# Forty scatters of a routed feed-forward layer, each to a view of its own

## The chip, the cores and the metric

The kernel runs on one core of a Trainium2 chip. The metric is the time of one execution on the device, in microseconds (us). Three runs of the kernel before took 685.83, 689.69 and 692.70 us; the median is 689.69 us. One further execution was profiled and took 693.05 us, of which the profile shows a span of 691.3 us.

The engines are PE (TensorE, matmul), ACT (ScalarE), DVE (VectorE), POOL (GpSimd) and SP (SyncE). POOL also issues every transfer whose addresses come from a table of indices, and one instruction after the other in the order in which the program has them.

## The reference

Attention comes first, for 8 batches of 8 heads, with 512 local queries (a band of 32 keys to either side and the 32 global keys) and 32 global queries. Its output is a matrix x of 4608 rows and 512 columns. Then each row goes to one of 8 experts:

```python
logits = x @ w_gate
# (row, expert) pairs in falling order of their logit: a row goes to the first
# expert that still has room; each expert takes cap = 4608 // 8 = 576 rows
for e in range(E):
    mask = assigned == e
    h = np.maximum(x[mask] @ w1[e], 0.0)     # 512 -> 1024
    out[mask] = h @ w2[e]                    # 1024 -> 512
```

Each row of `out` belongs to one expert, so the rows that two experts write are never the same, nor those of two tiles of one expert.

## The kernel before, in words

The first part, up to about 200 us, is attention; x goes to a buffer `xd` in DRAM. Then the rows of the first expert are chosen, and from about 238 us on the experts follow one after another. The experts are called phases 0 to 7 here, in the order in which they are worked on.

A phase has an H part and a Y part on PE. The H part (`ffn`, line 1127) multiplies the expert's 576 rows by W1: 16 pieces of 12 matmuls, each operand split in a high and a low half. ACT takes the relu (1129, 1131) and DVE the low half of it (`hl`, issued by line 1134 and recorded at 552). The Y part multiplies by W2: a tile of 32 rows (`rest_out`, 1094) and four tiles of 128 rows (`rows_out`, 1086). In phase 7 the small tile comes last, in the other phases first.

Each of the five tiles of a phase ends in `out_tile` (1069): ACT copies the sum to a buffer `y` (1074), and a scatter from POOL (`scatter`, 973 to 976) writes its rows to `out`, by a column of the table `idx`. So there are 8 x 5 = 40 scatters. The tiles of 128 rows are called s0 to s3 in this text. The 32-row tile is written as 128 pieces of 128 columns to `out4`, which is `out` seen as four times as many rows, a quarter as long.

POOL's other transfers in this part are gathers, all at line 918: the 576 rows of the next phase (`xg`, five of them), and its weights (`w1r` and `w2r`, two of 1 MB each). For each phase they stand in POOL's order so: five `xg`, two `w2r`, s0 to s3, two `w1r` for the phase after. At the turn from phase 5 to phase 6 it is different: s0, s1, the two `w1r` of phase 7, s2, s3, and then the five `xg` of phase 7.

The order on each engine is fixed when the program is built. The kernel counts a reckoned clock (`V.now`) along with PE's work, and a list `todo` holds jobs that are put into the program at the first step where that clock is late enough:

```python
def put():
    scatter(ph, t, y)
    wrote[0] = pool_op(1040, sizes[t] * 2048) + LAND
at("out", V.now + 900, put, lambda: V.now >= wrote[0])
```

So a scatter gets a place behind the point where the one before it is reckoned to have landed. Nothing of this runs on the chip. What runs there are waits on semaphores, which the program's dependency tracker adds: a scatter waits for the ACT copy of its own `y`, and, since all 40 write to one tensor with rows known only at run time, for the landing of a scatter before it.

Transfers issued by POOL count on eight semaphores in turn, DMASW0 to DMASW7. A transfer also waits until the last one on its own semaphore, eight transfers earlier, has landed, unless a wait before it already covers that.

Of the kernel before, what the change touches and what calls it, by code (L numbers as in the profile page):

```python
# [7 lines left out]

F32 = mybir.dt.float32
F32R = mybir.dt.float32r  # L10
# [11 lines left out]
E = 8  # L22
# [23 lines left out]
@with_exitstack  # L46
def block(ctx, tc, A, out, nbatch=B, dump=None):
    nc = tc.nc
    ctx.enter_context(tc.manual_schedule())
    consts = ctx.enter_context(tc.tile_pool(name="consts", bufs=1))  # L50
    dram = ctx.enter_context(tc.tile_pool(name="dram", bufs=1, space=DRAM))
    xd = dram.tile([N, DM], F32, name="xd")

    ident = consts.tile([128, 128], F32, name="ident")
    L = consts.tile([128, 34, E], F32, name="L")
    if dump is not None:
        nc.vector.memset(L, 0.0)
    rt = Routing(tc, A, consts, L, ident) if out is not None else None
    if rt:
        rt.begin(ctx)  # L60
    attention(tc, A, consts, xd, ident, L, nbatch, rt)
    if dump is not None:
        nc.sync.dma_start(dump["L"], L.rearrange("p a b -> p (a b)"))
        nc.sync.dma_start(dump["x"][:nbatch * S], xd[:nbatch * S])
    if out is not None:
        rt.begin_ps(ctx)
        experts(tc, A, xd, ident, rt, out)
# [830 lines left out]
def experts(ctx, tc, A, xd, ident, rt, out):  # L898
    nc = tc.nc
# [10 lines left out]
    hh = wp.tile([128, 8, CAP], F32R, name="hh")  # L910
    hl = wp.tile([128, 8, CAP], F32R, name="hl")
    h32 = wp.tile([128, 8, 32], F32, name="h32")
    out4 = out.rearrange("n (c d) -> (n c) d", c=4)
    sizes = [128, 128, 128, 128, 32]
    HF = CAP // 2

# [55 lines left out]

    def scatter(ph, t, y):
        k = t + (t == 4)
        nc.gpsimd.indirect_dma_start(out=out4 if t == 4 else out, out_offset=bass.IndirectOffsetOnAxis(  # L975
            ap=rt.idx[ph][:, k:k + 1], axis=0), in_=y, in_offset=None)

    V = rt.V
# [90 lines left out]
    def out_tile(ph, t, p):  # L1069
        while len([x for x in todo if x[0] == "out"]) > 3:  # L1070
            force("out", 1)
        w = 128 if t == 4 else DM
        y = st.tile([128, w], F32, name=f"y{w}", bufs=4 if w == DM else 2)
        nc.scalar.activation(y, p[:, :w], AF.Copy)  # L1074
# [5 lines that stand above are left out]
# [217 lines left out]
```

## Time and profile before

| | |
|---|---|
| median of 3 runs | 689.69 us (685.83 to 692.70) |
| profiled execution, own time | 693.05 us |
| its span | 691.3 us |
| PE busy | 644.5 us (93%) |
| DVE busy | 460.0 us (67%) |
| ACT busy | 307.4 us (44%) |
| POOL busy | 247.7 us (36%) |
| the 40 scatters, on POOL | 41.4 us, with 183.3 us of idle time ahead of them |

A chain of waits is followed back from the last instruction, and it gives PE 89% of the span. The idle time ahead of the scatters is POOL's own, and says nothing yet about PE. A wait for several semaphores is put down to the engine that came last by the profile, which is not always the one that was waited for: whoever reads a scatter's wait has to look at when its own `y` was ready.

### The profile page before, as it was taken

Reading aid. Unit: us, or ns where it says so; the run is one execution under the profiler, and the core shown is the slowest. Engines: PE = TensorE matmul, PEld = TensorE weight load, DVE = VectorE, ACT = ScalarE, POOL = GpSimd, SP = SyncE. Lnnn points to the kernel's source line nnn. Section 1 sums busy time; section 2 is a strip of 40 time slices with the busy share of each in tenths; the row PEclk is TensorE's granted clock in tenths of the full one; section 3 lists DMA queues with packets and bytes.
Section 4 is the critical chain, followed back from the end, with each engine's and each line's share of the span. In section 5 each row is a group of like instructions: output and inputs, shape, how many; then the busy total and the mean of one; then the engine's idle time right before and its main releaser. Section 6 shows DMA issues by size and latency. Waiting matters only on the chain.

```text
span 691.3 us, 24695 instructions
## 1 busy us (share of the span) xinstructions
PE 644.5 (93%) x10358; PEld 539.5 (78%) x10358; DVE 460.0 (67%) x1765; ACT 307.4 (44%) x828; POOL 247.7 (36%) x313
## 2 busy tenths in 40 slices
PE   7898999999973799999999999999999999999996
PEld 6576777776762698779879879878978978988985
DVE  4688888788776699778758758767767772640410
ACT  5777867876720252443433324334333342542410
POOL 4687767786500311511421331141151133412011
PEclk9999999999985799999999999999999999999999
DMA  8677778876210531713240450361343146431001
GB/s 252 192 241 221 228 227 249 256 212 185 90 68 2 186 124 42 287 47 109 84 168 18 153 190 33 126 197 53 122 125 129 45 142 214 163 127 49 14 15 51
DMA packets 41119, 93.91 MB, mean 136 GB/s; under 512 B 5424, under 2 KB 28208, under 8 KB 36912
## 3 DMA queue, kind: packets, MB, share of 16 engines
q0 software_dynamic: 10240, 51.39, 21.5%
q1 hardware_dynamic: 30768, 40.95, 19.5%
q8 instruction: 81, 1.33, 0.8%
q14 instruction: 30, 0.25, 0.1%
HBM read 74.49 MB, written 17.83 MB: 134 GB/s over the span
## 4 chain that ended last, share of the span: by engine, by line
PE 89%; DVE 4%; issue 3%; DMA 2%; ACT 1%; SPq 0%; POOL 0%; POOLq 0%; ACTq 0%
PE H L1127 28%; PE Y L1086 27%; PE T L90 11%; PE S L90 7%; PE O L90 7%; PE R L630 4%; PE H L965 2%; PE Y L1094 2%; DMA qk<-in_qk_dram 1%; DVE r_pm L552 1%; DMA mask<-in_mask_dram 1%; DMA xg<-xd,idx 0%; DVE r_G L552 0%; DVE r_ce L552 0%; DMA out_dram<-y,idx 0%
## 5 line engine op out<-in xcount | busy, mean ns | idle before, releaser
L1127 PE MATMUL H<-xh,w1h 128*128 128x272 f32 (+2 forms) x512 | 151.1, 295 | 2.4 <-ACT xh L970 2.0
L1127 PE MATMUL H<-xh,w1l 128*128 128x272 f32 (+2 forms) x512 | 150.4, 294 | 0.0
L1127 PE MATMUL H<-xl,w1h 128*128 128x272 f32 (+2 forms) x512 | 149.7, 292 | 0.1
L975 POOL DMA_INDIRECT out_dram<-y,idx x40 | 41.4, 1036 | 183.3 <-ACT y L1074 102.8
L1086 PE MATMUL Y<-w2l,hh 128*128 128x512 f32 x256 | 103.3, 403 | 0.8 <-issue 0.8
L1129 ACT ACTIVATE hh<-H 128x272 fp32r<-128x272 f32 (+2 forms) x128 | 50.8, 398 | 119.7 <-PE H L1127 117.0
L1086 PE MATMUL Y<-w2h,hh 128*128 128x512 f32 x256 | 104.0, 406 | 0.0
L1086 PE MATMUL Y<-w2h,hl 128*128 128x512 f32 x256 | 103.4, 404 | 0.0
L1127 PEld LDWEIGHTS H<-xh,w1h 128*128 128x128 f32 x512 | 97.0, 189 | 3.9 <-ACT xh L970 2.1
L1127 PEld LDWEIGHTS H<-xl,w1h 128*128 128x128 f32 x512 | 97.0, 189 | 1.0 <-DVE xl L552 0.4
L1127 PEld LDWEIGHTS H<-xh,w1l 128*128 128x128 f32 x512 | 97.0, 189 | 0.4
L126 POOL COPY vw<-vw 32x650 f32<-32x650 f32 x96 | 69.4, 723 | 51.6 <-DMA vw<-in_vw_dram 36.1
L180 ACT ACTIVATE p<-p,nm 128x128 f32<-128x128 f32 x256 | 78.0, 397 | 8.1 <-DVE nm L175 8.1
L1074 ACT ACTIVATE y<-Y 128x512 f32<-128x512 f32 (+1 forms) x40 | 21.3, 534 | 123.7 <-PE Y L1086 80.3
L552 DVE SCALAR_TENSOR_TENSOR hl<-H,hh 128x272 fp32r<-128x272 f32 (+2 forms) x128 | 55.1, 434 | 30.3 <-ACT h L1131 18.5
L175 DVE CUSTOM_DVE_ANT_0 p<-S,mask 128x128 f32<-128x128 f32 x256 | 56.5, 286 | 23.3 <-PE S L90 21.8
L90 PE MATMUL S<-qk 64*32 64x128 f32 (+2 forms) x2240 | 52.6, 293 | 9.5 <-issue 5.1
L552 DVE TENSOR_TENSOR w2l<-w2r,w2h 128x512 fp32r<-128x512 f32 x64 | 42.8, 682 | 25.3 <-ACT w2h L931 25.3
L918 POOL DMA_INDIRECT xg<-xd,idx x40 | 43.3, 1082 | 38.1 <-DVE idx L552 23.8
L1086 PEld LDWEIGHTS Y<-w2h,hh 128*128 128x128 f32 x256 | 48.2, 188 | 10.4 <-issue 1.4
L1086 PEld LDWEIGHTS Y<-w2h,hl 128*128 128x128 f32 x256 | 48.2, 188 | 9.8 <-issue 0.5
L1086 PEld LDWEIGHTS Y<-w2l,hh 128*128 128x128 f32 x256 | 48.2, 188 | 9.5 <-issue 0.4
(179 smaller groups left out, 1116.9 us busy)
## 6 DMA issues: line engine op xcount, KB each, us to landing
qk<-in_qk_dram SPq DMA_DIRECT2D x64, 204.0 KB, 2.9
vw<-in_vw_dram SPq DMA_DIRECT2D x64, 162.5 KB, 3.4
xd<-xs SPq DMA_DIRECT2D x28, 256.0 KB, 3.5
qk<-in_qk_dram SPq DMA_DIRECT2D x32, 200.0 KB, 3.0
xd<-xs SPq DMA_DIRECT2D x1, 1024.0 KB
xg<-xd,idx POOLq DMA_INDIRECT x40
out_dram<-y,idx POOLq DMA_INDIRECT x40
vw<-in_ve_dram SPq DMA_DIRECT2D x32, 16.2 KB, 3.0
```

The source lines that it names most:

```text
L90: s.last = op(o, w, x, **kw)
L126: copy(bv[32 * g:32 * g + 32], av[32 * g + 32:32 * g + 64])
L175: nc.vector.tensor_tensor_reduce(s.p[:, c, :], s.st[:, c, :], mask[:, c, :], -SCALE, BIG, ALU.add, ALU.min, s.nm[:, c:c + 1])
L180: nc.scalar.activation(s.p[:, c, :], s.p[:, c, :], AF.Exp, bias=s.nm[:, c:c + 1], scale=-1.0)
L552: return op(*args, **kw)
L630: s.nc.tensor.matmul(out, *args, **kw)
L918: nc.gpsimd.indirect_dma_start(out=dst, out_offset=None, in_=src, element_offset=off, in_offset=bass.IndirectOffsetOnAxis(ap=idx, axis=0))
L975: nc.gpsimd.indirect_dma_start(out=out4 if t == 4 else out, out_offset=bass.IndirectOffsetOnAxis(ap=rt.idx[ph][:, k:k + 1], axis=0), in_=y ...
L1074: nc.scalar.activation(y, p[:, :w], AF.Copy)
L1086: nc.tensor.matmul(p, h[:, f, q], w[f], start=(f + k == 0), stop=(f + k == 9))
L1127: nc.tensor.matmul(p, w[d][:, fs], x[:, d, q], start=(d + k == 0), stop=(d + k == 5))
L1129: nc.scalar.activation(hh[:, f, q], p, AF.Relu)
```

## The change

The 40 scatters no longer name `out`. `dram_disjoint_views(out, 5 * E)` makes 40 views of the whole tensor, and scatter t of phase ph writes to view 5 * ph + t; the dependency tracker takes it that no two of them overlap. The rows that are written, the tables, the buffers, the reckoned spacing and the sizes stay.

```diff
+from concourse.bass_types import dram_disjoint_views
...
-    out4 = out.rearrange("n (c d) -> (n c) d", c=4)
+    outs = dram_disjoint_views(out, 5 * E)
...
     def scatter(ph, t, y):
         k = t + (t == 4)
-        nc.gpsimd.indirect_dma_start(out=out4 if t == 4 else out, out_offset=bass.IndirectOffsetOnAxis(
+        o = outs[5 * ph + t]
+        if t == 4:
+            o = o.rearrange("n (c d) -> (n c) d", c=4)
+        nc.gpsimd.indirect_dma_start(out=o, out_offset=bass.IndirectOffsetOnAxis(
             ap=rt.idx[ph][:, k:k + 1], axis=0), in_=y, in_offset=None)
```

No instruction that works or transfers changes its place on any engine; on PE, DVE, ACT and SP the waits stay as well. POOL's waits are what changes. At the end of the program, phase 7's five scatters (128 rows each, then the tile of 32 as 128 pieces) stood so on POOL:

```order
L975 DMA out_dram<-y_11839,idx 4352x512 [waits DMASW3_49,DMASW2_49,Activation_49]
L975 DMA out_dram<-y_11867,idx 4352x512 [waits DMASW4_49,DMASW3_49,Activation_49]
L975 DMA out_dram<-y_11895,idx 4352x512 [waits DMASW5_49,DMASW4_49,Activation_49]
L975 DMA out_dram<-y_11923,idx 4352x512 [waits DMASW5_49,Activation_49]
L975 DMA out_dram<-y_11959,idx 17408x128 [waits DMASW6_49,Activation_49]
```

Here DMASW5 in the fourth row and DMASW6 in the fifth are the scatter just before. The same five now:

```order
L979 DMA out_dram<-y_11839,idx 4352x512 [waits DMASW3_49,Activation_49]
L979 DMA out_dram<-y_11867,idx 4352x512 [waits DMASW4_49,Activation_49]
L979 DMA out_dram<-y_11895,idx 4352x512 [waits DMASW5_49,Activation_49]
L979 DMA out_dram<-y_11923,idx 4352x512 [waits DMASW6_49,Activation_49]
L979 DMA out_dram<-y_11959,idx 17408x128 [waits DMASW7_49,Activation_49]
```

Each waits for its own `y` and for its own semaphore's last user, eight transfers earlier. At the turn from phase 5 to phase 6 (s0, s1, W1 of phase 7, s2, s3, the rows of phase 7) POOL had:

```order
L975 DMA out_dram<-y_10879,idx 4352x512 [waits DMASW1_49,Activation_49]
L975 DMA out_dram<-y_10947,idx 4352x512 [waits DMASW2_49,DMASW1_49,Activation_49]
L918 DMA w1r<-in_w_dram,widx 128x2048 [waits DMASW3_49,DVE_49]
L918 DMA w1r<-in_w_dram,widx 128x2048 [waits DMASW4_49,DVE_49]
L975 DMA out_dram<-y_11038,idx 4352x512 [waits DMASW5_49,DMASW2_49,Activation_49]
L975 DMA out_dram<-y_11066,idx 4352x512 [waits DMASW6_49,DMASW5_49,Activation_49]
L918 DMA xg<-xd,idx 128x512 [waits DMASW7_49,DVE_49]
L918 DMA xg<-xd,idx 128x512 [waits DMASW0_49,PE_49]
L918 DMA xg<-xd,idx 128x512 [waits PE_49] x2
L918 DMA xg<-xd,idx 32x512 [waits DMASW3_49,PE_49]
```

And now:

```order
L979 DMA out_dram<-y_10879,idx 4352x512 [waits DMASW1_49,Activation_49]
L979 DMA out_dram<-y_10947,idx 4352x512 [waits DMASW2_49,Activation_49]
L919 DMA w1r<-in_w_dram,widx 128x2048 [waits DMASW3_49,DVE_49]
L919 DMA w1r<-in_w_dram,widx 128x2048 [waits DMASW4_49,DVE_49]
L979 DMA out_dram<-y_11038,idx 4352x512 [waits DMASW5_49,Activation_49]
L979 DMA out_dram<-y_11066,idx 4352x512 [waits DMASW6_49,Activation_49]
L919 DMA xg<-xd,idx 128x512 [waits DMASW7_49,DVE_49]
L919 DMA xg<-xd,idx 128x512 [waits DMASW0_49,PE_49]
L919 DMA xg<-xd,idx 128x512 [waits DMASW1_49,PE_49]
L919 DMA xg<-xd,idx 128x512 [waits DMASW2_49,PE_49]
L919 DMA xg<-xd,idx 32x512 [waits DMASW3_49,PE_49]
```

The second semaphore of s1, s2 and s3 is gone, and the middle `xg` gathers, which had been covered by those waits, wait for DMASW1 and DMASW2 (s0 and s1) themselves.

## Rows read from the trace of the kernel before

**Rows 1.** The page: busy time, share, instructions of each engine.

```profile
PE 644.5 (93%) x10358; PEld 539.5 (78%) x10358; DVE 460.0 (67%) x1765; ACT 307.4 (44%) x828; POOL 247.7 (36%) x313
```

**Rows 2.** Stretches of the experts' part: length, busy us by engine, clock, DMA; all eight's sum.

```profile
255.00:303.60 48.60, 46.43 (x508) 37.49 (x507) 39.41 (x115) 17.89 (x42) 15.39 (x14) 1.00 0.35 128
...
sum 428.20, PE 425.24 PEld 365.56 DVE 267.71 ACT 151.56 POOL 105.26; mean PE 53.16 PEld 45.70 DVE 33.46 ACT 18.94 POOL 13.16
```

**Rows 3.** Line 975, the 40 scatters: durations; POOL's idle time before them, by releaser.

```profile
L975 POOL DMA_INDIRECT out_dram<-y,idx x40: 967/992/1446, 275.1 to 687.6; - x40
...
  issue: 45.0, 16
  DMA out_dram<-y,idx: 12.9, 3
```

**Rows 4.** POOL in time, phase 2: start, length, instruction, idle before and releaser.

```profile
402.57 1.01 POOL L975 DMA_INDIRECT out_dram<-y,idx  x1 [0.30 <-issue]
411.39 1.23 POOL L975 DMA_INDIRECT out_dram<-y,idx  x1 [7.81 <-DMA out_dram<-y,idx]
415.13 0.97 POOL L975 DMA_INDIRECT out_dram<-y,idx  x1 [2.51 <-issue]
...
435.19 0.98 POOL L918 DMA_INDIRECT w1r<-in_w_dram,widx  x1 [15.41 <-DVE r_a L552]
```

**Rows 5.** ACT in time, phase 2: the copies of two tiles.

```profile
401.36 0.59 ACT L1074 ACTIVATE y<-Y 128x512 f32<-128x512 f32 x1
...
408.33 0.60 ACT L1074 ACTIVATE y<-Y 128x512 f32<-128x512 f32 x1 [2.51 <-issue]
```

**Rows 6.** POOL in time, the turn from phase 5 to phase 6.

```profile
573.07 1.13 POOL L975 DMA_INDIRECT out_dram<-y,idx  x1 [0.30 <-issue]
581.61 0.99 POOL L975 DMA_INDIRECT out_dram<-y,idx  x1 [7.41 <-ACT y L1074]
582.90 0.98 POOL L918 DMA_INDIRECT w1r<-in_w_dram,widx  x1 [0.30 <-issue]
...
595.73 0.99 POOL L975 DMA_INDIRECT out_dram<-y,idx  x1 [7.34 <-ACT h L1131]
597.02 0.98 POOL L918 DMA_INDIRECT xg<-xd,idx  x1 [0.30 <-issue]
```

**Rows 7.** ACT in time, the same turn: tile s3's copy and the conversion of W2.

```profile
585.66 0.60 ACT L1074 ACTIVATE y<-Y 128x512 f32<-128x512 f32 x1 [5.01 <-PE Y L1086]
586.15 2.18 ACT L931 ACTIVATE w2h<-w2r 128x512 fp32r<-128x512 f32 x4
```

**Rows 8.** The chain that ended last: start, length, what; the first is phase 6.

```profile
612.09 2.30 PE Y L1086 x9
614.39 0.44 PE H L965 x4
```

**Rows 9.** DVE in time, phase 2: the operation that ran into the scatter at 411.39.

```profile
411.07 0.69 DVE L552 TENSOR_TENSOR w1l<-w1r,w1h 128x512 fp32r<-128x512 f32 x1
```

**Rows 10.** The page: the costliest groups, one of that shape on DVE: busy us, mean ns.

```profile
L552 DVE TENSOR_TENSOR w2l<-w2r,w2h 128x512 fp32r<-128x512 f32 x64 | 42.8, 682 | 25.3 <-ACT w2h L931 25.3
```

**Rows 11.** ACT and POOL in time, the program's last 9 us.

```profile
683.24 0.60 ACT L1074 ACTIVATE y<-Y 128x512 f32<-128x512 f32 x1 [4.96 <-PE Y L1086]
684.11 0.97 POOL L975 DMA_INDIRECT out_dram<-y,idx  x1 [4.59 <-ACT y L1074]
685.65 0.28 ACT L1074 ACTIVATE y<-Y 128x128 f32<-128x128 f32 x1 [1.81 <-PE Y L1094]
687.59 0.97 POOL L975 DMA_INDIRECT out_dram<-y,idx  x1 [2.51 <-DMA out_dram<-y,idx]
```

**Rows 12.** Line 1293, the program's end: durations in ns, first and last start.

```profile
L1293 SPq EVENT_SEMAPHORE  x11: 17/28/28, 689.9 to 691.2; - x11
```

## The prediction, on record before the result was known

> **What bounds the kernel now.** I read the page first, for who is busy. PE is, with 644.5 of 691.3 us [rows 1]. So a wait on POOL is worth something only if PE, or the end of the program, waits for what it holds up. The table of stretches says how much PE could still give back in the experts' part, the only part with scatters. In the eight stretches from 255 us to PE's last large matmul at 683.2, PE is busy for 425.24 of 428.20 us [rows 2]. It stands idle for 2.96 us, of which 48.60 - 46.43 = 2.17 lie in the first stretch, so 0.79 are left for the other seven.
>
> Then the scatters' own line. Of POOL's idle time ahead of them, 45.0 + 12.9 = 57.9 us in 19 waits has a landing, or nothing that the profile names, as its end [rows 3]. Timelines of POOL and ACT show what ended such a wait. In phase 2 the copy of tile s1 ended at 401.36 + 0.59 = 401.95 [rows 5], and s0 left POOL at 402.57 + 1.01 = 403.58 [rows 4]. Yet s1 went out at 411.39. Nothing is left that it can have waited for but the landing of s0, for 7.81 us. s2's copy ended at 408.93 [rows 5], and s2 went out at 415.13, 2.51 us behind s1 [rows 4]: again a landing. So these waits are real, and large. The reader is to see that they are POOL's alone: the next thing on POOL waits 15.41 us more for DVE's routing [rows 4].
>
> Last the end of the program, where POOL is what everything waits for [rows 11, 12].
>
> **The change, part by part.** It moves no instruction. It takes waits from the scatters of 128 rows and from the last one of 32, and puts some waits on gathers.
>
> *Scatters in the middle of a phase.* Without the landing, s1 of phase 2 leaves 0.30 us (the usual step between two of POOL's transfers) behind s0: 403.58 + 0.30 = 403.88, 7.5 us sooner. s2 leaves behind its copy at about 409.2, 5.9 us sooner. What comes next on POOL, the W1 gather, waits for `r_a` until 435.19 whatever the scatters do [rows 4]. The `y` buffers come free sooner, and no copy waits for one (each copy's `y` was last used a phase earlier). Worth: 0. The cover is the 15.41 us ahead of the W1 gather; without it a gather would be up to 7.8 us sooner.
>
> *The turn from phase 5 to 6.* Here gathers stand behind scatters, so they move. s1 leaves at 573.07 + 1.13 + 0.30 = 574.50 in place of 581.61, and W1 of phase 7 at 574.50 + 0.99 + 0.30 = 575.79 in place of 582.90 [rows 6]. s3's copy ends at 586.26 [rows 7]; with 0.27 us from ACT to POOL (below) it leaves at 586.53 in place of 595.73, and the first gather of phase 7's rows at 587.82 in place of 597.02 [rows 6]. That is 9.2 us sooner. But PE turns those rows at 614.39, and gets there straight from the matmul before, which ends at 612.09 + 2.30 = 614.39 [rows 8]. They were in time already. Worth: 0.
>
> *The last scatter.* The 32-row tile's copy ends at 685.65 + 0.28 = 685.93; its scatter goes out at 687.59, 2.51 us after s3's issue was done at 685.08 [rows 11]. Freed, it needs only its copy. From a copy to its scatter POOL took 684.11 - (683.24 + 0.60) = 0.27 us one tile earlier [rows 11]. So it leaves at 685.93 + 0.27 = 686.20, and 687.59 - 686.20 = 1.39 us are gained. What follows, landing until about 689.9 [rows 12] and the closing waits to 691.27, starts with the issue and moves with it. Worth: -1.39, the only term on the path. What is late next is the copy itself, so PE and ACT.
>
> *Waits added.* A gather of `xg` now waits for a scatter of the phase before. In phase 2 three of its four large scatters have gone out by 415.13, and the gathers that will wait for them stand behind the W1 gather of 435.19 [rows 4], 20 us later, where the longest landing seen took 8 us. At the turn the third and fourth `xg` wait for s0 and s1, which leave by 574.50 and land by about 581.6 (the old s1 waited for s0 until then), and the gathers are not due before 587.8. Worth: 0.
>
> *POOL beside DVE.* The freed scatters are issued at other moments, some beside DVE. The row for this: the scatter at 411.39 took 1.23 us, the quiet one after it 0.97 [rows 4]. DVE's operation that ran into it took 0.69 [rows 9], and the mean of that shape is 0.682 [rows 10]. So POOL lost 0.26 us and DVE 0.01. I price it at 0, since POOL has idle time and PE does not wait for POOL. The Trainium skill, page "SBUF — State Buffer", section "SBUF: two separate sides", says that GpSimd cannot write a transfer's descriptors while VectorE runs an operation on both ports of the pair that they share. By that rule alone the scatters would be longer, not PE's work, and the sum would be the same; that the holding goes the other way too is a rival below.
>
> *Sum.* 0 + 0 - 1.39 + 0 + 0 = -1.39 us. The profiled execution's own time of 693.05 becomes 691.66. It stood 3.36 above the median of 689.69; from the median the forecast is 688.30 us, 0.2% faster.
>
> **The rivals.**
>
> *Nothing is gained at the end.* The last scatter leaves sooner, but its data queue behind s3's, and landings keep the pace of one after another. Then the time stays at 693.05, or 689.69 from the median. For it: s1 of phase 2 waited 7.81 us for a landing while others wait 2.51 [rows 4], so transfers do queue behind earlier ones. Against it: at the end only s3's 256 KB are ahead, and it has been out since 685.08.
>
> *PE's pauses go too.* The gathers at the turn come sooner, scatters no longer bunch, and all 2.96 us of PE's idle time vanish [rows 2]. Then 1.39 + 2.96 = 4.35 are gained: 688.70, or 685.34 from the median. Against it: 2.17 of them lie before 303.6, where routing for the first phases runs. Even this, the most that the rows allow, is 0.6%.
>
> *Slower: DVE is held by POOL.* In phases 1 to 5 s1 now goes out right behind s0, where DVE works on the routing whose small matmuls stand in PE's order among the Y tiles. If a scatter's issue held DVE's operation for its whole 0.97 us, and PE, which takes its instructions in order, waited for just that operation, each phase would lose 0.97: 5 x 0.97 - 1.39 = +3.46, so 696.51, or 693.15 from the median. With s2 and s3 caught as well, 15 x 0.97 - 1.39 = +13.2. It decides from 1.39 / 5 = 0.28 us a phase on. For it: the scatter beside DVE got longer, so the two do meet; the skill's page calls that port pair an exclusive lock. Against it: DVE's own operation kept its time [rows 9, 10], and PE lost only 0.79 us in all of seven stretches [rows 2] in which every gather is issued beside the same work.
>
> *The change doesn't do what it says.* In the built program's order the landing is gone from the scatters' waits at all places that I name, so this gets no chance of its own.
>
> **How the numbers follow.** The forecast gets 0.85, nothing gained 0.07, the pauses 0.04, slower 0.04. About 1% (6.9 us) is what a measurement of this kernel can tell from no change. None of the first three cases leaves that band. The slower one does with nearly two scatters caught in each phase, a quarter of its chance. What is left, 0.03 to each side, comes from the runs themselves, which lay 1.0% apart. Faster 0.03, within 1% 0.93, slower 0.04. For the range I take the runs seen, shifted by the term: 685.83 - 1.39 = 684.4 and 692.70 - 1.39 = 691.3. The upper end goes to 692.0, half of the way to the slowest run with nothing gained (692.7); the pauses' 685.3 lies inside, the slower case's 693.2 outside.
>
> **What would show it.** Right: s1 of phases 1 to 5 about 0.3 us behind s0; the 19 waits on landings gone from the scatters' line; PE busy for 425 of some 428 us in the same stretches; W1 of phase 7 gathered some 7 us sooner beside an unmoved PE; the last scatter 0.3 us behind its copy, and the span's end 691.3 - 685.93 - 1.39 = 4.0 us behind that copy in place of 5.4. Wrong: PE pauses at routing matmuls in phases 1 to 5, DVE rows longer than before beside scatters, or a last scatter that leaves at once and still lands 3.7 us later or more.

## The result, and the profile after

Fifteen runs of the change have a median of 693.52 us (690.92 to 698.39), fifteen of the kernel before 689.34 us (685.83 to 692.70). The ratio is 1.0057, with a 95% interval of 1.0036 to 1.0077. The forecast was 688.3 us with 692.0 as its upper end, so the sign is wrong: where 1.39 us should have been gained, some 4 were lost. The profiled execution took 693.52 us, with a span of 691.7.

The scatters did what was foreseen. Their waits on landings are gone; what is left ahead of them is mostly the wait for their own `y` (before: [rows 3]). The row has the instruction, its count, busy us and mean ns, then POOL's idle time before it and what ended most of it:

```profile
L979 POOL DMA_INDIRECT out_dram<-y,idx x40 | 41.8, 1044 | 162.3 <-ACT y L1078 153.2
```

The end of the program is shorter, too. ACT and POOL in time, the last 7 us (before: [rows 11]):

```profile
685.11 0.60 ACT L1078 ACTIVATE y<-Y 128x512 f32<-128x512 f32 x1 [4.96 <-PE Y L1090]
685.99 0.97 POOL L979 DMA_INDIRECT out_dram<-y,idx  x1 [4.59 <-ACT y L1078]
687.49 0.28 ACT L1078 ACTIVATE y<-Y 128x128 f32<-128x128 f32 x1 [1.78 <-PE Y L1098]
688.04 0.97 POOL L979 DMA_INDIRECT out_dram<-y,idx  x1 [1.08 <-ACT y L1078]
```

The last scatter leaves 0.27 us behind its copy (687.77), and the span's end stands 3.9 us behind that copy where it stood 5.4.

The loss lies in the middle. The same eight stretches as in [rows 2], two of them and the sum (length, busy us of PE, PEld, DVE, ACT, POOL, clock, DMA):

```profile
417.50:474.40 56.90, 56.38 (x569) 47.90 (x568) 39.81 (x116) 20.56 (x51) 14.38 (x14) 1.00 0.32 110
...
531.20:588.00 56.80, 55.06 (x527) 46.90 (x526) 34.54 (x104) 18.87 (x48) 15.62 (x15) 1.00 0.43 152
...
sum 428.20, PE 422.58 PEld 363.26 DVE 265.76 ACT 150.25 POOL 105.25; mean PE 52.82 PEld 45.41 DVE 33.22 ACT 18.78 POOL 13.16
```

PE is busy for 2.66 us less than before (425.24). Measured from the first matmul of a phase to the first of the next, phases 1 to 5 took 57.23, 56.62, 56.97, 56.78 and 56.85 us before, and take 58.11, 57.23, 57.75, 57.21 and 58.63 now: 4.48 us more. Phase 6 took 51.28 and takes 51.09; phase 7 with the end took 54.58 and takes 53.14. Phases 1 to 7 together are 2.85 us longer. The medians differ by 4.18 us; what is left of that lies outside what these two profiles show, whose phase 0 took 63.31 us before and 61.13 after.

To see what PE waits for, take one place, the routing inside the Y part of phase 3. PE sums digits (`R<-r_oh`, then `R<-rem`), DVE makes `r_ce` from that sum, and PE needs `r_ce` some matmuls later. Before, all engines in time, without the Y matmuls:

```profile
460.76 1.01 POOL L975 DMA_INDIRECT out_dram<-y,idx  x1 [0.30 <-issue]
...
460.89 0.17 PE L630 MATMUL R<-rem,one 128*32 128x16 f16 x1
...
463.01 0.42 DVE L552 TENSOR_TENSOR r_ce<-R,dk 128x256 f16<-128x256 f32 x1 [3.50 <-PE H L965]
...
464.18 0.28 PE L630 MATMUL R<-r_ce,big 128*128 128x128 f16 x2
```

And after:

```profile
459.82 1.01 POOL L979 DMA_INDIRECT out_dram<-y,idx  x1 [0.30 <-issue]
459.92 0.17 PE L631 MATMUL R<-rem,one 128*32 128x16 f16 x1
...
461.13 0.99 POOL L979 DMA_INDIRECT out_dram<-y,idx  x1 [0.30 <-issue]
463.40 0.43 DVE L553 TENSOR_TENSOR r_ce<-R,dk 128x256 f16<-128x256 f32 x1 [4.84 <-remote]
463.46 0.28 ACT L932 ACTIVATE xh<-H 128x128 fp32r<-128x128 f32 x1 [3.18 <-remote]
...
463.88 0.27 PE L631 MATMUL R<-r_ce,big 128*128 128x128 f16 x2 [0.47 <-DVE r_ce L553]
```

The reader is to see three things. `r_ce` lasts as long as before (0.43 us against 0.42). But it starts 463.40 - 460.09 = 3.31 us behind the matmul that it waits for, where it started 463.01 - 461.06 = 1.95 behind; ACT, which waits for another matmul (`H<-ident,xg`), starts late at the same moment. And both starts lie 1.2 to 1.3 us behind the end of POOL's unbroken series of issues, which ended with s0 before (461.77) and ends with s1 now (462.12). Before, 0.75 us were left between the end of `r_ce` and PE's use of it (463.43 to 464.18); 1.3 us more is too much, and PE stands idle for 0.47 us. Phases 1, 2 and 4 show the same: starts 3.25 to 3.29 us behind in place of 1.95 to 2.07, and pauses of 0.43 to 0.47 us at the same matmul.

In phase 5 W1 of phase 7 follows s1, and PE pauses later, at the digit sums that stand behind the turning of the small tile of rows (573.0 to 579.6 us, all engines):

```profile
574.54 0.43 PE L966 MATMUL H<-ident,xg 32*128 32x32 f32 x4
574.57 0.99 POOL L979 DMA_INDIRECT out_dram<-y,idx  x1 [0.30 <-ACT xh L932]
...
575.86 0.98 POOL L919 DMA_INDIRECT w1r<-in_w_dram,widx  x1 [0.30 <-issue]
576.62 0.28 ACT L932 ACTIVATE xh<-H 128x128 fp32r<-128x128 f32 x1 [2.07 <-remote]
...
578.72 0.19 PE L631 MATMUL R<-r_ohl,rhs 128*32 128x64 bf16 x1 [0.45 <-issue]
579.42 0.28 PE L631 MATMUL R<-r_ohl,rhs 128*32 128x64 bf16 x9 [0.51 <-issue]
```

ACT's copy `xh` of that tile starts 1.65 us behind the matmul that it waits for. Set beside each other matmul for matmul, the two phases 5 drift apart by 1.34 us at these digit sums and by 0.42 earlier, where PE waits for a landing of `xg`. That wait is not the change's: among the runs below, h1, without late signals, has 1.1 us of it, and f2, the kernel before, 1.1 too.

### The profile page after: what moved, and what is told of

It reads as the page before. It is cut to its first block, busy times and chain, and to the rows that moved or that the text cites. A ratio compares the mean times of both kernels' runs of the same rounds, so it can differ in the third digit from the quotient of the medians.

```text
span 691.7 us, 24718 instructions
## 1 busy us (share of the span) xinstructions
PE 647.0 (94%) x10358; PEld 542.0 (78%) x10358; DVE 460.0 (67%) x1765; ACT 307.5 (44%) x828; POOL 247.7 (36%) x313
## 4 chain that ended last, share of the span: by engine, by line
PE 75%; issue 11%; DVE 7%; another core or an unknown queue 3%; ACT 1%; POOL 1%; DMA 1%; POOLq 0%; ACTq 0%
PE H L1131 25%; PE Y L1090 15%; PE T L91 12%; PE S L91 7%; PE O L91 7%; PE R L631 4%; PE Y L1098 2%; PE H L966 1%; POOL out_dram L979 1%; PE Y L1164 1%; DVE r_pm L553 1%; DMA xg<-xd,idx 1%; DVE r_ce L553 1%; DVE r_G L553 1%
## 5 line engine op out<-in xcount | busy, mean ns | idle before, releaser
L919 POOL DMA_INDIRECT w1r<-in_w_dram,widx x16 | 15.6, 977 | 122.1 <-DVE r_a L553 92.2
```

The lines of the kernel that those rows point to most:

```text
L919: nc.gpsimd.indirect_dma_start(out=dst, out_offset=None, in_=src, element_offset=off, in_offset=bass.IndirectOffsetOnAxis(ap=idx, axis=0))
```

## The experiments

Theory A, from these rows: while POOL issues a series of transfers, PE's signals reach their waiters late, and s1 makes the series longer. Theory B: s1's 256 KB on their way do it. Theory D: some other freed or added wait costs. Theory C came with the second group of runs: whether signals are late depends on the chip on which a kernel runs.

The trace records semaphore updates. I call a signal late when its update stands over 0.5 us behind the end of the instruction that makes it. In the seven profiles with late signals some updates have no record (9 to 13 of PE's 894, 15 to 17 of ACT's 761, 25 to 33 of DVE's 1415); in the other thirteen all have one. So records and instructions are paired in order, such that the delays are least in sum.

Late signals are then PE's alone. No recorded update of ACT or DVE stands more than 0.02 us behind in any profile. Those without a record were in time wherever a waiter shows it, with few exceptions: set against a like program without late signals, the waiter starts as soon, within 0.03 us, for 23 of 23 of ACT's and 76 of 80 of DVE's. Where an expectation below speaks of late signals of ACT and DVE, a missing record was taken for a late one.

Every late signal comes while POOL issues a transfer or within 1.6 us of the end of an issue. Not every signal there is late: in the change's first profile 66 matmuls that signal end inside an issue, and 18 of their signals are late, 37 in time, 11 without a record.

All results in one table; kernels of one group ran on one chip, beside runs of the kernel before on it. No numbered chip comes twice, and that of the first group is not on record. "late" counts PE's late signals; "1-4" is the sum of phases 1 to 4 in the profile, "7" is phase 7 with the end, both in us.

| group, chip | kernel | ratio (95%) | late | 1-4 | 5 | 6 | 7 |
|---|---|---|---|---|---|---|---|
| first | before | 1 | 33 | 227.60 | 56.85 | 51.28 | 54.58 |
| | the change | 1.0057 (1.0036-1.0077) | 28 | 230.30 | 58.63 | 51.09 | 53.14 |
| second, 3 | e1, s1 held | 0.9974 (0.9953-0.9996) | 0 | 227.46 | 56.73 | 50.71 | 52.64 |
| | e2, last alone | 0.9982 (0.9959-1.0006) | 0 | 227.36 | 56.99 | 50.71 | 52.64 |
| | e3, s1 alone | 1.0019 (0.9999-1.0039) | 0 | 227.41 | 56.54 | 50.72 | 54.56 |
| | e4, s1 behind `r_ce` | 0.9966 (0.9941-0.9991) | 0 | 227.45 | 57.02 | 50.69 | 52.63 |
| third, 9 | f1, the change | 1.0071 (1.0044-1.0099) | 33 | 230.94 | 58.89 | 51.25 | 53.18 |
| | f2, before | 1.0019 (0.9989-1.0048) | 31 | 228.01 | 57.74 | 51.88 | 54.57 |
| | f3, extra gather | 1.0038 (1.0006-1.0070) | 28 | 230.45 | 57.18 | 52.28 | 54.34 |
| | f4, s1 alone | 1.0063 (1.0034-1.0093) | 30 | 230.45 | 56.36 | 50.72 | 54.58 |
| fourth, 2 | g1, the change | 0.9971 (0.9945-0.9998) | 0 | 227.34 | 57.16 | 50.72 | 52.64 |
| | g2, s1 held | 0.9978 (0.9957-0.9999) | 0 | 227.44 | 56.41 | 50.69 | 52.64 |
| | g3, s1 held, copy | 0.9963 (0.9943-0.9983) | 0 | 227.42 | 56.59 | 50.72 | 52.62 |
| | g4, s1 behind `r_ce` | 0.9982 (0.9959-1.0005) | 0 | 227.40 | 56.92 | 50.71 | 52.63 |
| fifth, 14 | h1, s1 held | 0.9971 (0.9944-0.9999) | 0 | 227.43 | 57.70 | 50.72 | 52.63 |
| | h2, s1 held, copy | 0.9988 (0.9960-1.0015) | 0 | 227.42 | 56.68 | 50.69 | 52.63 |
| | h3, s1 behind `r_ce` | 0.9969 (0.9948-0.9990) | 0 | 227.44 | 57.25 | 50.71 | 52.65 |
| sixth, 6 | i1, s1 held | 1.0000 (0.9978-1.0022) | 29 | 227.72 | 56.86 | 52.28 | 53.16 |
| seventh, 0 | j1, last alone | 1.0006 (0.9981-1.0031) | 0 | 227.42 | 56.37 | 50.72 | 52.63 |
| | j2, s1 held, copy | 0.9964 (0.9937-0.9990) | 0 | 227.44 | 57.76 | 50.72 | 52.62 |

Phase 5 lasts 56.37 to 57.76 us without any late signal, with the wait for `xg` in it, so a difference of 1 us in it says little by itself. The kernel before had medians of 687.93, 687.94, 687.55 and 688.13 us in the groups without late signals, and of 689.34, 692.47 and 690.21 in those with them.

**Second group.** e1 is the change, but s1 shares s0's view and so waits for its landing:

```diff
-        o = outs[5 * ph + t]
+        o = outs[5 * ph + (0 if t == 1 else t)]
```

> The change, but s1 shares the view of s0, so s1 alone waits for s0's landing again; s2, s3, the small tile and the last scatter stay free. Theory A (POOL's issue of s1 right behind s0 lengthens an unbroken series of transfers, and PE's completion signals do not get through until it is over, so the routing on DVE and with it PE come late): the phase lengths 1 to 5, from a phase's first H matmul to the next phase's, go back to 57.2, 56.6, 57.0, 56.8, 56.9 us from 58.1, 57.2, 57.8, 57.2, 58.6, the end stays 1.4 us shorter; 0.998 of before. Theory B (the data of s1 moving beside the W2 gathers delays something): the same. Theory D (the waits that the change adds to gathers, or s2 and s3, cost the time): stays at 1.005 to 1.006.

e2 frees the last scatter alone (two views):

```diff
-        o = outs[5 * ph + t]
+        o = outs[(ph, t) == (E - 1, 4)]
```

> Only the last scatter of the program is freed, all others wait as before. All theories: phases 0 to 6 as before, the span ends 4.0 us behind the last copy of y in place of 5.3, 0.998 of before. If the end were bound by something else: 1.000.

e3 frees s1 of phases 1 to 4 alone (two views):

```diff
-        o = outs[5 * ph + t]
+        o = outs[t == 1 and 0 < ph < 5]
```

> Only s1 of phases 1 to 4 is freed, everything else waits as before, the end and the turn from phase 5 to 6 too. Theories A and B: phases 1 to 4 longer by 0.9, 0.6, 0.8, 0.4 us as in the changed kernel, phase 5 and the end as before; +2.7 us, 1.004 of before. Theory D: 1.000.

e4 is the change with a wait for DVE's first `r_ce`, in phases 1 to 5 (the text below says 1 to 4):

```diff
+            s.first = v if it == 0 else s.first
...
+        if t == 1 and 0 < ph < 6:
+            tc.add_manual_dep(d.ins, rt.first.ins.name, ...)
```

> The change, but s1 of phases 1 to 4 waits until DVE's first r_ce of the routing is done, not for a landing; it then leaves some 2 us later than in the changed kernel and some 5 us before s0 has landed. Theory A: phases 1 to 4 as long as before (57.2, 56.6, 57.0, 56.8), phase 5 as in the changed kernel (58.6, about +1.8), the end 1.4 us shorter: together +0.4, 1.000 to 1.001 of before. Theory B: s1's data still move beside the W2 gathers, so phases 1 to 4 stay long, +3.1 us, 1.0045.

Theory A fell in the form in which it stood here. In e3 s1 left right behind s0, and phases 1 to 4 lasted as long as in the kernels beside it; no signal was late in any of the four. e3 gave 1.0019 where theories A and B had 1.004, and e4 0.9966 where A had 1.000 to 1.001 and B 1.0045. So either the traces of this chip differ, or the programs do. The next group put the change and the kernel before on one chip with two others.

**Third group.** f1 and f2 are the change and the kernel before, word for word; f4 is e3 again. f3 is the kernel before with a gather of 64 KB behind s0:

```diff
+    spare = wp.tile([128, 128], F32, name="spare")
...
+            if t == 0 and 0 < ph < 5:
+                gather(spare, xd.rearrange("n (c d) -> (n c) d", c=4), 0, rt.idx[ph][:, :1])
```

> The change, word for word, once more, beside the other three kernels of this group. Theory C (PE's late signals belong to the execution or to the chip it runs on, not to the program): where the profile shows PE's signals on time, phases 1 to 5 last 57.2, 56.6, 57.0, 56.6 and 56.9 us as in the four experiments before, the end is 1.4 us shorter than that of the kernel before, and the time is 1 to 3 us below it (ratio 0.996 to 0.999). Theory A (the series of s0 and s1 in one piece holds PE's signals whenever it stands in the change as a whole): phases 1 to 5 are 0.4 to 1.8 us longer again, ratio 1.004 to 1.008.

> The kernel before, once more, for a profile of the same group. Theory C: if the change's profile of this group shows PE's signals on time, this one does too (PE's signal within 0.02 us of the matmul's end while POOL issues), with phases 1 to 5 near 57.2, 56.6, 57.0, 56.6 and 56.9 us; if there they are late, here they are late too. Theory A: signals are late in the series of s0, some 1.2 us behind its end, as in the first profile. Its ratio is 1 within 0.2% under both.

> The kernel before, with in phases 1 to 4 one more gather of 64 KB into a spare tile, issued by POOL right behind s0; all waits of before are kept. Theory A: POOL's series is 1 us longer there, PE's signals come 1 us later, and phases 1 to 4 are 0.4 to 0.9 us longer each, 2 to 3 us in all (ratio 1.003 to 1.005). Theory C: the same where the profiles of this group show late signals; where they are on time, phases 1 to 4 are unchanged within 0.1 us and the ratio is 1 within 0.2%.

> The kernel before with s1 of phases 1 to 4 alone sent to a second view, so that it leaves right behind s0; the last scatter waits as before. It gave 1.0019 (0.9999 to 1.0039) before, with phases 1 to 4 at 57.2, 56.6, 57.0 and 56.6 us in the profile. Theory A: 1.003 to 1.006. Theory C: as the other profiles of this group show PE's signals: on time, 1 within 0.2% and the same phases; late, phases 1 to 4 longer by 0.4 to 0.9 us each and 1.003 to 1.005.

Here signals were late in all four, and the loss was back. f3, phase 3, as above:

```profile
460.93 0.17 PE L630 MATMUL R<-rem,one 128*32 128x16 f16 x1
...
462.12 0.98 POOL L919 DMA_INDIRECT spare<-xd,idx  x1 [0.30 <-issue]
464.47 0.42 DVE L552 TENSOR_TENSOR r_ce<-R,dk 128x256 f16<-128x256 f32 x1 [4.91 <-remote]
464.54 0.28 ACT L932 ACTIVATE xh<-H 128x128 fp32r<-128x128 f32 x1 [2.40 <-remote]
464.81 0.68 DVE L552 TENSOR_TENSOR xl<-H,xh 128x512 fp32r<-128x512 f32 x1
464.95 0.27 PE L630 MATMUL R<-r_ce,big 128*128 128x128 f16 x2 [0.54 <-DVE r_ce L552]
```

No scatter is moved in f3; the transfer in s1's place reads DRAM where s1 writes it, and has a quarter of its bytes. Yet `r_ce` starts 464.47 - 461.10 = 3.37 us behind its matmul and 1.37 behind the end of POOL's series (f4: 3.44 and 1.42), and phases 1 to 4 sum to 230.45 us in f3 as in f4, 2.44 more than in f2. So one more transfer issued by POOL costs it, a gather of 64 KB as well as a scatter of 256 KB. That speaks against theory B, and against any story of scatters that meet in DRAM. So does the trace of before: the signals held behind s0 came by 463.06 us, and those of the next two matmuls, which end at 464.46 and 465.20, came 0.01 us behind, while the DMA engines were busy for 93% of the time from 463.06 to 466.70 and s0 had not landed before 466.7. By its ratio f3 (1.0038, from 1.0006 to 1.0070) is not clear of f2 (1.0019); its phases carry the argument. The phases explain 2.4 us of f4's loss, which by its ratio is 4.4 (2.4 to 6.4).

**Fourth group.** g1 is the change a third time, g2 is e1 and g4 is e4 again. g3 is e1 with a copy of s1's `y` by SP, to put the bytes beside the routing without an issue by POOL:

```diff
+    scr = [dr.tile([128, DM], F32, name=f"scr{i}") for i in range(4)]
...
+        if t == 1 and 0 < ph < 5:
+            nc.sync.dma_start(scr[ph - 1], y)
```

> The change a third time. So far: 1.0057 and 1.0071 in two groups whose profiles show the signals of PE, ACT and DVE up to 3 us late while POOL issues; in a third group, whose profiles show no late signal, s1 alone gave 1.0019. Theory C (the loss is the late signals, which some chips show and others do not): late signals in this group's profiles, phases 1 to 5 longer by 0.4 to 1.8 us and 1.004 to 1.008; none, phases 1 to 5 at 57.2, 56.6, 57.0, 56.6 and 56.9 us, the end 1.4 us shorter, and 0.996 to 0.9995. Theory A (the loss is in the program, on every chip): 1.004 to 1.008 either way.

> The change, but s1 goes to s0's view and so waits for s0's landing as before; the other scatters are free. It gave 0.9974 where no signal was late. Theory C: late signals in this group, phases 1 to 4 within 0.2 us of the kernel before, phase 5 too, the end 1.4 us shorter, 0.996 to 0.9995; none, the same. The change beside it is then slower by 0.5 to 0.9% if signals are late, and equal within 0.2% if not.

> The kernel of the run ahead with, in phases 1 to 4, a copy of y of s1 (256 KB) to spare DRAM issued by SP as soon as y of s1 is there, so that a transfer of that size runs beside the routing without an issue by POOL. Theory A and C: the loss is tied to POOL's issue, so equal to the run ahead within 0.2% and no signal late at another place. Theory B (a transfer of that size beside the routing is what costs): phases 1 to 4 longer by 0.4 to 0.8 us each, 0.3 to 0.4% above the run ahead.

> The change with one wait more: s1 of phases 1 to 5 leaves once DVE's first r_ce of the routing is done (some 2 us later than in the change, 0.3 us ahead of the kernel before). It gave 0.9966 where no signal was late. Theory C, late signals: the routing starts as in the kernel before, phases 1 to 4 within 0.3 us of it, phase 5 in between, 0.996 to 1.001; no late signals: 0.996 to 0.999. Theory A: as theory C with late signals, on every chip.

No signal was late, and the same change is faster. Phase 3 of g1:

```profile
458.88 1.01 POOL L979 DMA_INDIRECT out_dram<-y,idx  x1 [0.30 <-issue]
458.99 0.17 PE L631 MATMUL R<-rem,one 128*32 128x16 f16 x1
459.23 0.42 DVE L553 TENSOR_TENSOR r_ce<-R,dk 128x256 f16<-128x256 f32 x1 [1.62 <-PE R L631]
...
460.19 0.99 POOL L979 DMA_INDIRECT out_dram<-y,idx  x1 [0.30 <-issue]
462.27 0.28 PE L631 MATMUL R<-r_ce,big 128*128 128x128 f16 x2
```

POOL issues s0 and s1 as it did in the first profile, but `r_ce` starts 0.07 us behind its matmul, in the midst of s0's issue, and is done 2.62 us before PE needs it. The copy of g3 cost nothing here, which does not tell what it does where signals are late.

**Fifth to seventh group.** h1 and i1 are e1, h2 and j2 are g3, h3 is e4, j1 is e2. They were to show on a chip with late signals what is left when s1 is held.

> The change with s1 in s0's view, so that it waits for s0's landing as before. 0.9974 and 0.9978 where no signal is late. Theory C, late signals in this group's profile: phases 1 to 4 within 0.2 us of the kernel before, the end 1.4 us shorter, ratio 0.996 to 0.9995. If the other scatters that were set free cost something beside late signals (theory D): 1.000 to 1.004, with phases 1 to 5 longer at other places. No late signals: 0.996 to 0.9995 under both.

> The run ahead with the copy of 256 KB from y of s1 to spare DRAM by SP in phases 1 to 4. 0.9963 where no signal is late. Late signals, theory C (the loss is tied to POOL's issue): equal to the run ahead within 0.3%, and no engine's signal late at the copy. Theory B (the traffic of s1 delays the signals): signals late behind the copy's issue too, phases 1 to 4 longer by 0.4 to 0.8 us, 0.3 to 0.4% above the run ahead.

> The change, with s1 of phases 1 to 5 leaving behind DVE's first r_ce. 0.9966 and 0.9982 where no signal is late. Late signals, theory C: r_ce starts some 1.2 us behind the end of s0's issue as in the kernel before; phases 1 to 4 within 0.3 us of it, ratio 0.996 to 1.001. Theory D (any scatter into the routing costs there, wherever it stands): 1.003 to 1.006.

> The change with s1 in s0's view, so that it waits for s0's landing as before. 0.9974, 0.9978 and 0.9971 where no signal is late. Theory C, late signals in this profile: phases 1 to 4 within 0.2 us of the kernel before, the end 1.4 us shorter, ratio 0.996 to 0.9995. Theory D (the other scatters set free cost something beside late signals): 1.000 to 1.004. No late signals: 0.996 to 0.9995 under both.

> The kernel before with the last scatter alone sent to a second view. 0.9982 (0.9959 to 1.0006) where no signal is late. Theory C with late signals: phases 1 to 6 as in the kernel before there (57.2, 56.6 to 56.8, 57.0, 56.8 to 57.0, 56.9 to 57.7, 51.3 to 51.9), the end 1.4 us shorter, 0.996 to 0.9995, below the change with s1 held (1.000) by the turn's 0.4 to 1.0 us. No late signals: 0.996 to 0.9995 too.

> The change with s1 held, and a copy of 256 KB from y of s1 to spare DRAM issued by SP in phases 1 to 4. 0.9963 and 0.9988 where no signal is late. Late signals: if they are tied to POOL's issue (theory C), phases 1 to 4 stay within 0.3 us of 57.2, 56.65, 57.3 and 56.5, ratio 0.998 to 1.002. If the traffic of s1 does it (theory B), phases 1 to 4 are 0.4 to 0.8 us longer each, ratio 1.002 to 1.006.

Only i1 met late signals. j1, the last scatter alone, gave 1.0006 (0.9981 to 1.0031) where I had expected 0.996 to 0.9995. Phase 3 of i1:

```profile
458.29 1.01 POOL L979 DMA_INDIRECT out_dram<-y,idx  x1 [0.31 <-issue]
458.39 0.17 PE L631 MATMUL R<-rem,one 128*32 128x16 f16 x1
...
460.48 0.42 DVE L553 TENSOR_TENSOR r_ce<-R,dk 128x256 f16<-128x256 f32 x1 [3.46 <-PE H L966]
460.55 0.28 ACT L932 ACTIVATE xh<-H 128x128 fp32r<-128x128 f32 x1 [1.71 <-PE H L966]
...
461.71 0.29 PE L631 MATMUL R<-r_ce,big 128*128 128x128 f16 x2
```

With s1 back behind s0's landing, `r_ce` starts 1.92 us behind its matmul as in the kernel before, phases 1 to 4 are 227.72 us (phase 3 alone 57.30, 0.33 more than in the first profile of before) and phase 5 is 56.86: theory C for the middle. The end's gain is there, and yet the ratio is 1.000 (0.9978 to 1.0022), above the 0.996 to 0.9995 that I expected and at the lower end of what theory D allows. Phase 6 took 52.28 us; in the two profiles of the kernel before it took 51.28 and 51.88, but 52.28 in f3 too, where the turn was left alone. So that this gave the gain back is not shown. Nor is it settled what the bytes of s1 alone do where signals are late, since h2 and j2 met none.

## Why the prediction was wrong, point by point

*What bounds the kernel: right.* PE does, and the scatters' waits were POOL's alone. Where no signal is late, taking them away changes nothing in phases 1 to 4: 227.34 us in the change (g1), 227.36 where the middle is as before (e2).

*Scatters in the middle, turn, added waits, each worth 0: right as waits.* s1 left 0.30 us behind s0. At the turn W1 left at 575.86, where 575.79 was forecast, and phase 6 lost nothing by it (51.28 and 51.09; 51.88 and 51.25).

*The last scatter, -1.39: right.* Phase 7 with the end became 1.44 us shorter in the first pair and 1.39 in the third group. In the whole time it does not show by itself: e2 gave 0.9982 and j1 1.0006, with 1 inside both intervals. Where no signal is late it is 52.64 where the last scatter is free (g1) and 54.56 where it waits (e3): 1.92. The rest comes from the copy, which starts sooner there. g1's end, ACT and POOL:

```profile
680.87 0.60 ACT L1078 ACTIVATE y<-Y 128x512 f32<-128x512 f32 x1 [4.96 <-PE Y L1090]
681.74 0.97 POOL L979 DMA_INDIRECT out_dram<-y,idx  x1 [4.59 <-ACT y L1078]
682.74 0.28 ACT L1078 ACTIVATE y<-Y 128x128 f32<-128x128 f32 x1 [1.27 <-PE Y L1098]
683.29 0.97 POOL L979 DMA_INDIRECT out_dram<-y,idx  x1 [0.57 <-ACT y L1078]
```

The last copy begins 1.00 us behind the start of s3's issue (681.74), and 1.87 behind the copy before it; in the change's first profile it is 1.50 and 2.38. So in the first profile the signal of PE's last matmuls was held beside s3's issue (0.55 us behind, at 687.46), and the 0.5 us come off the same path.

*POOL beside DVE, priced 0: this step failed.* I asked whether an operation of DVE gets longer while POOL issues, found 0.69 against 0.682 us [rows 9, 10], and took that for the whole price. The price lies ahead of the operation: it starts late, and a duration does not show that. The trace of before did. The line of `r_ce` in the table of DVE's groups, before (busy us, mean ns; then DVE's idle time before it, with its releasers):

```profile
L552 DVE TENSOR_TENSOR r_ce<-R,dk 128x256 f16<-128x256 f32 (+1 forms) x56 | 22.7, 405 | 37.1 <-PE R L630 22.4 <-PE H L965 14.2
```

After, and in g1:

```profile
L553 DVE TENSOR_TENSOR r_ce<-R,dk 128x256 f16<-128x256 f32 (+1 forms) x56 | 22.6, 404 | 41.9 <-PE R L631 21.2 <-remote 19.4 <-PE H L966 0.7
```

```profile
L553 DVE TENSOR_TENSOR r_ce<-R,dk 128x256 f16<-128x256 f32 (+1 forms) x56 | 22.7, 405 | 25.7 <-PE R L631 25.1
```

`r_ce` reads R and has no need of H, and still 14.2 us of its idle time were put down to H before: it began behind a later instruction than the one it waits for. The timeline of before gives both sizes: 460.89 + 0.17 = 461.06 to 463.01 is the delay, 463.43 to 464.18 the 0.75 us of cover that was left. The step should have been: s1 behind s0 makes POOL's series 1.3 us longer, so `r_ce` comes 1.3 later, and PE loses, by this estimate, 1.3 - 0.75 = 0.55 us in each of phases 1 to 4. Measured are 2.70 / 4 = 0.68 in the first pair, and 2.93 / 4 = 0.73 in the third group. Set beside each other phase by phase, PE's matmuls of phase 3 in the two traces keep their distance up to the first use of `r_ce`, are 0.63 us late from there, and 0.78 from the second. At the turn two W1 gathers follow s1 as well, and the same step missed 1.34 us of phase 5 in the first pair and 1.68 in the third group, at the digit sums. PE pausing at routing matmuls was among the prediction's own signs of being wrong. In the fourth group, without late signals, the price was indeed 0: the change gave 0.9971, some 2.0 us (0.1 to 3.8) less, where 1.39 were forecast.

*The slower rival* had the place and almost the size: s1 behind s0 in phases 1 to 5, 693.15 us where 693.52 were measured. The size was partly luck, 0.97 us for each phase, where they lost 0.88, 0.61, 0.78, 0.43 and 1.78. Its mechanism was another, a DVE operation held for the length of an issue. What I held against it, that DVE's operation kept its time, was true and beside the point. My other argument, that PE lost only 0.79 us in seven stretches, told that the cover was enough before, not how much of it was left. The page of the Trainium skill that I weighed there ("SBUF — State Buffer", "SBUF: two separate sides") speaks of a lock between GpSimd and VectorE; here the late signals were PE's, `r_ce` on DVE kept its length, and s1's issue took 0.99 us in the first profile of the change as in g1, without late signals. The page "Perfetto Trace Analysis" of the Trainium skill, section "Tensor Engine Instruction (MATMUL, LD_WEIGHTS)", would have been the one to weigh: the end that a profile gives a matmul is an estimate, and the signal goes out only after the write is acknowledged, and then has to reach the others. It gives no time for it. This case's traces do: `r_ce` starts 0.07 us behind in g1, and 1.86 to 3.55 at this place of phases 1 to 4 in the seven profiles with late signals.

*The range* rested on the three runs of before, shifted. It had no room for a cost that one group of runs shows and another does not.

## What to carry to other kernels

Before giving an issuing engine work earlier, look at who waits for a signal beside the longer series: take the start of the waiting operation minus the end of what it waits for, and the cover between its end and its first use; a duration shows neither. Holding back the one transfer that lengthens the series, and freeing the rest, is what these runs suggest: with s1 held the change gave 0.9971 to 0.9978 in three groups without late signals and 1.000 in one with them, while the change itself gave 0.9971 in one group without and 1.0057 and 1.0071 in two with them. The two were not run side by side where signals are late; there the saving rests on the phases of i1. A difference of half a per cent is to be seen on more than one chip before it is believed, of either sign.

## What the runs showed of the hardware

In three of the seven groups signals of PE reach their waiters as much as 3.5 us behind the matmul's end, while POOL issues transfers or shortly after; in the other four they don't, for the same program: 28 and 33 late ones in two profiles of the change, 0 in the third. No recorded signal of ACT, DVE or POOL was more than 0.02 us behind. Within a group the profiles always agreed. An extra gather of 64 KB did as much as a scatter of 256 KB.

What makes the groups differ stays open: no numbered chip was met twice, so the chip can't be told from the occasion. So does what in POOL's issue holds a signal, and why a third of PE's signals inside an issue are late and most are not. Records of updates are missing in the profiles with late signals and in no others; whether the profiler's recording has a part in the delay was not tested.

In the groups with late signals the kernel before itself is slower, with medians of 689.34 to 692.47 us against 687.55 to 688.13.
